# Retention, routed experts and a dense block on one core: where the query decay is multiplied in, which banks the transposes own, when the embedding is normalised, and how tiles are grouped

## The chip, the core and the metric

The kernel runs on one core of a Trainium2 chip. The core's engines run their own instruction queues in order: TensorE (PE, with its weight loads PEld), VectorE (DVE), ScalarE (ACT), GpSimd (POOL) and SyncE (SP, which here only issues transfers). An instruction starts when those ahead of it on its engine are done and the semaphores that it waits on have been raised. The metric is the time of one execution on the device in microseconds (us), as a median of several runs.

## The reference

Three stages follow each other. Stage one is a retention layer without softmax, for 4 batches, 8 heads, 576 positions and a head size of 64. The score of query position i and key position j is multiplied by a decay, gamma of the head to the power i - j:

```
scores = scale * np.matmul(q, k.transpose(0, 1, 3, 2))
gamma = 1.0 - 2.0 ** (-5.0 - np.arange(H, dtype=np.float32))
Dmat = np.where(rel >= 0, gamma[:, None, None] ** rel[None, :, :], 0.0)
ret = scores * Dmat[None, :, :, :]
return np.matmul(ret, v).astype(np.float32)
```

Its output, 2304 rows of 512, goes to stage two, which sends each row to one of 8 experts: the row and the 8 expert embeddings are normalised, the logits are their products divided by tau, the largest picks the expert, and its softmax weight scales the row's result `relu(x @ w1[e]) @ w2[e]`. Stage three is a dense block over all rows, `elu(x @ w_in) @ w_out`, whose weights come as float64.

## The kernel before, in words

**Decay as two factors.** gamma ** (i - j) is split into gamma ** i on the query and gamma ** -j on the key. Two constant tables of 5 position groups by 8 heads, `gq` and `gk`, hold them.

**Units and tiles.** The first stage runs over ten units (`UNITS`), each a pair of rows of work: per pair of batches four units of 256 positions (two tiles of 128 rows of output, two "slots") and one remnant unit (positions 512 to 575 of both batches, one tile, one slot). In units 0 to 9 the remnants are 4 and 9. There are 18 tiles.

**What a unit does.** The loop over `u` near line 684 issues, in this order: POOL scales q and k of unit u+2 (`scale`, L276); SP loads q, k of unit u+4 and v of u+3 (`load`, L257, L261); PE multiplies the carried state (`carried`, L340) and the scores of the second slot (`scores`, L315), DVE masks them (L320); PE transposes slot 0 of q and k of the next unit (`transposes`, L290), ACT copies each out of PSUM (L298); PE projects the previous unit's second tile (`xrows`, L404, "xa") with an identity matrix that also carries the expert embeddings, so that 128 columns are the row itself and 8 are logits; a pump of small DVE steps for the routing; transposes of slot 1; the product with v (`values`, L353), copied by ACT (L359, "xT"); the next unit's first scores; the state update (`summed`, L373, DVE L380 to L386); the projection of the unit's first tile; again a pump.

**PSUM.** Eight banks: `sc0`, `sc1` one each; `T`, `X`, `Y` two each. `T` holds a pair, q's transpose in its first bank and k's in its second, and also half of the projections; it has one buffer.

**Evicting a projection.** With tag `T` ACT copies the row (L416) and the logits (L418) and DVE sums the logits (L408); with tag `Y` DVE does both (L421, L408). SP stores the row in DRAM (L429) and ACT sums its squares for the norm (L441).

**Routing.** Tiles form four groups (`GROUPS`, 5 5 5 3). When a group's last tile is projected, two generators of small DVE steps (`expert_steps`, L473 to L534, and `gate_steps`, L445 to L562) are put into the pump, which stops at each `STEP`: a PE product "rp" (L490) in the one, an ACT exponential "ex" (L549) in the other. POOL then builds selection tables (L572 to L575) for each tile of a finished group. The last group is handled after the loop, in a serial tail up to the first product of the experts (L944).

**Start.** Before the loop, DVE scales unit 0, PE transposes it, ACT squares the embeddings (L625), DVE normalises them (L445 to L631), PE computes the first scores and state, and `emb_end` (L641) swaps halves of the embeddings (L645) and transposes them into the projection's matrix (L650).

**Rest.** From the first expert product to the end PE works through experts and the dense block with float32 operands split in two parts; the change does not touch that.

Of the kernel before, what the change touches and what calls it, by code (L numbers as in the profile page):

```python
# [17 lines left out]
P = 128  # L18
# [22 lines left out]
GROUPS = [(0, 5), (5, 5), (10, 5), (15, 3)]  # L41
# [4 lines left out]
for _n, _w in (("gq", 5 * H), ("gk", 5 * H), ("id", 2 * NT), ("w8", 8), ("base", 8), ("lim", NE * NK), ("i24", 24),  # L46
               ("i128", P), ("mask0", P), ("mask1", P), ("maskr", 64), ("lower", P)):
    COL[_n] = (_o, _o + _w)
    _o += _w
# [4 lines left out]
def constants():  # L54
# [10 lines left out]
    put("gq", (g[None, None, :] ** at[:, :, None] / 8.0).reshape(P, -1))  # L65
# [18 lines left out]
def tile_kernel(ctx: ExitStack, tc: tile.TileContext, q, k, v, emb, tau, w1, w2, w_in, w_out, const, out):  # L84
# [156 lines left out]
    rhsx = [st.tile([P, KD, P + NE], F32, name=f"rhsx{j}") for j in range(2)]  # L241
# [39 lines left out]
    def transposes(u, s_):  # L281
        if u >= NU or s_ not in slots_of(u):
            return
        if s_ == 0:
            tT[u] = (a2.tile([P, 4, 2, P], F32, tag="qTs", name=f"qT{u}"), a2.tile([P, 4, 2, 2, 64], F32, tag="kTs", name=f"kT{u}"))
        pair = ps.tile([P, 2, 512], F32, tag="T", name=f"qkT{u}_{s_}")
        for j, nm in enumerate("qk"):
            pt = pair[:, j].rearrange("p (r b i) -> p r b i", r=4, b=2)
# [3 lines left out]
            if j:  # L292
# [101 lines left out]
    def xrows(n, tag):  # L394
# [5 lines left out]
        xa = ps.tile([P, 2, 512], F32, tag=tag, name=f"xa{n}")  # L400
        W = P + NE
        for pr in range(4):
            for u, b, p0, w in where[n]:
                nc.tensor.matmul(xa[p0:p0 + w, pr // 2, (pr % 2) * W:(pr % 2 + 1) * W], xTs[u][b][:, pr, :w], rhsx[b][:, pr, :], start=True, stop=True)  # L404
        xav = xa[:, :, :2 * W].rearrange("p a (b w) -> p a b w", b=2)
        xs = xss[n] = a2.tile([P, 2, 2, P], F32, tag="xs", name=f"xs{n}", bufs=3)
        def logits(src):
            vec.tensor_reduce(out=gt[gi]["lg"][:, n - g0], in_=src, axis=AX.XY, op=ALU.add)  # L408

        le = xav[:, :, :, P:]  # L410
        if n == NT - 1:
            logits(le.rearrange("p a b e -> p e a b"))
            for a in range(2):
                nc.scalar.copy(out=xs[:, a], in_=xav[:, a, :, :P])
        elif tag == "T":
            nc.scalar.copy(out=xs, in_=xav[:, :, :, :P])  # L416
            lt = a2.tile([P, 2, 2, NE], F32, tag="lt", name=f"lt{n}")
            nc.scalar.copy(out=lt, in_=le)  # L418
            logits(lt.rearrange("p a b e -> p e a b"))
        else:  # L420
            vec.tensor_copy(out=xs, in_=xav[:, :, :, :P])  # L421
            logits(le.rearrange("p a b e -> p e a b"))
        b, c = TILES[n]
# [4 lines left out]
        for p0, p1, t0, eng in spans:  # L428
            eng.dma_start(out=xd[t0:t0 + p1 - p0, :], in_=xs[p0:p1].rearrange("p a b w -> p (a b w)"))  # L429

    xss = {}
# [5 lines left out]
    def squares(n):  # L437
        gi = grp_of[n]
        g0 = GROUPS[gi][0]
        sq = a2.tile([P, 2, 2, P], F32, tag="sq", name=f"sq{n}", bufs=1)  # L440
        nc.scalar.activation(out=sq, in_=xss[n], func=AF.Square, accum_out=gt[gi]["ss"][:, n - g0:n - g0 + 1])  # L441
# [148 lines left out]
    gcols = COL["gk"][1]  # L590
# [8 lines left out]
    for kk in range(KD):  # L599
        pool.tensor_copy(out=rhsx[0][:, kk, :P], in_=ident)  # L600
        for j in range(2):
            pool.tensor_copy(out=rhsx[1][:, kk, 64 * j:64 * j + 64], in_=ident[:, 64 - 64 * j:P - 64 * j])
# [3 lines left out]
    nc.scalar.dma_start(out=em, in_=emb)  # L606
    nc.scalar.dma_start(out=rtau, in_=tau.partition_broadcast(P))
    nc.sync.dma_start(out=ct[:, gcols:], in_=const[:, gcols:CSMALL])
    load(1, "v")
    load(2, "qk")  # L610
    scale(0)
    scale(1)
    for s_ in range(2):
# [7 lines left out]
    e1 = st.tile([NE, DM], F32, name="e1")  # L621
    es = st.tile([NE, 4], F32, name="es")

    def emb_steps():
        nc.scalar.activation(out=e1, in_=em, func=AF.Square, accum_out=es[:, 0:1])  # L625
        vec.reciprocal(out=rtau, in_=rtau)
        yield
        yield from norm_steps(es[:, 0:1], es[:, 1:2], es[:, 2:3])
        vec.reciprocal(out=es[:, 3:4], in_=es[:, 2:3])
        yield  # L630
        vec.tensor_scalar(out=e1, in0=em, scalar1=es[:, 3:4], scalar2=rtau[:NE, 0:1], op0=ALU.mult, op1=ALU.mult)  # L631
        yield

    for _ in emb_steps():
        pass
    scores(0, 0)
    summed(0)
    load(2, "v")
    load(3, "qk")

    def emb_end():  # L641
        pe = ps.tile([P, 2, KD, NE], F32, tag="Y", name="pemb")
        swap = st.tile([NE, KD, 2, 64], F32, name="swap")
        for j in range(2):
# [828 lines left out]
```

## Time and profile before

| what | us |
|---|---|
| median of 3 runs (786.06, 789.69, 790.55) | 789.69 |
| the profiled execution, whole | 785.31 |
| the profiled execution, span of the trace | 783.2 |
| PE busy in the span | 721.8 (92%) |
| DVE busy | 584.4 (75%) |
| ACT busy | 454.3 (58%) |
| POOL busy | 252.0 (32%) |

The profiled execution's time is 2.1 us longer than its span; what is before the first and after the last instruction stays. Busy shares are means over stages with different limits, so the first stage is read by itself: start of the span to about 167.6 us, where the first expert product begins. [...] In a row of the timeline, the bracket gives the time that the engine sat idle before the instruction, and what released it.

### The profile page before, as it was taken

What the parts mean: (1) busy time and instruction counts of PE and PEld (TensorE: products, weight loads), DVE (VectorE), ACT (ScalarE), POOL (GpSimd) and SP (SyncE); (2) the same over time, 40 slices, a digit from 0 to 9 for tenths busy, and PEclk for the clock granted to TensorE, in tenths of its full rate; (3) what the DMA queues carried; (4) which work ended last, traced back from release to release, by engine and by line L of the source; (5) the groups of instructions that cost most, each with busy time, mean ns of one, the idle gap of its engine ahead of it and who ended that gap; (6) DMA issues with size and microseconds to landing.
All of it is one profiled execution on the core that took longest, in us unless ns stands there. A gap on an engine that the chain in (4) does not pass through costs nothing.

```text
span 783.2 us, 15397 instructions
## 1 busy us (share of the span) xinstructions
PE 721.8 (92%) x5882; PEld 663.9 (85%) x5882; DVE 584.4 (75%) x917; ACT 454.3 (58%) x704; POOL 252.0 (32%) x370
## 2 busy tenths in 40 slices
PE   5687768589999999999899999999999999999996
PEld 5576667469999999998898899988999898989995
DVE  3335655577778879986888989998778998777773
ACT  2144434335565666565667766787665777676662
POOL 4314634341399124110052232227212324421103
PEclk8799889889999999999999999999999999999999
DMA  9575824157879999989733322114412123322102
GB/s 258 114 216 151 217 82 163 56 157 247 291 267 297 328 292 290 303 293 333 239 133 104 115 91 92 57 55 161 162 54 72 63 82 108 105 61 77 28 28 80
DMA packets 101794, 123.78 MB, mean 158 GB/s; under 512 B 12202, under 2 KB 71886, under 8 KB 101718
## 3 DMA queue, kind: packets, MB, share of 16 engines
q1 hardware_dynamic: 97430, 111.71, 45.6%
q0 software_dynamic: 3104, 9.83, 3.7%
q10 hardware_dynamic: 1184, 1.24, 0.6%
q8 instruction: 47, 0.77, 0.4%
q14 instruction: 29, 0.24, 0.1%
HBM read 99.91 MB, written 22.85 MB: 157 GB/s over the span
## 4 chain that ended last, share of the span: by engine, by line
issue 24%; PE 16%; POOL 9%; DVE 4%; DMA 1%; ACT 1%; POOLq 0%; ACTq 0%; DVEq 0%
PE o L229 6%; PE X L229 3%; PE Y L229 3%; PE h L229 2%; POOL out_dram L1385 2%; POOL qs L1187 2%; POOL qs L1186 2%; POOL qs L1184 2%; PE acc L961 2%; POOL qa L1185 1%; DMA ra<-in_moe_w_dram 1%; PE acc L963 1%; DVE hA L1350 0%; DVE glA L1358 0%; DVE xA L1347 0%
## 5 line engine op out<-in xcount | busy, mean ns | idle before, releaser
L1184 POOL TENSOR_TENSOR qs<-qa 128x256 f32<-128x256 f32 x24 | 22.4, 935 | 251.3 <-DMA qa<-wd 49.9
L229 PE MATMUL h<-xth,ha 128*128 128x332 f32 (+7 forms) x252 | 74.4, 311 | 1.0 <-DVEq L1094 1.0
L961 PE MATMUL acc<-hh,hb 128*128 128x342 f32 (+7 forms) x256 | 73.6, 304 | 1.7 <-ACT hh L947 1.7
L961 PE MATMUL acc<-hh,lb 128*128 128x342 f32 (+7 forms) x256 | 73.6, 303 | 0.3 <-DVE lb L203 0.3
L229 PE MATMUL h<-xtl,ha 128*128 128x332 f32 (+7 forms) x252 | 72.3, 303 | 0.0
L947 ACT ACTIVATE hh<-h 128x342 fp32r<-128x342 f32 (+7 forms) x64 | 27.1, 424 | 45.6 <-PE h L229 43.4
L320 DVE TENSOR_TENSOR A<-sc,ctbig 128x512 f32<-128x512 f32 (+1 forms) x36 | 22.1, 653 | 42.1 <-PE sc L315 42.1
L1337 ACT ACTIVATE rA<-hA 128x768 f32<-128x768 f32 x24 | 20.4, 848 | 55.3 <-DVE hA L1330 55.3
L203 DVE TENSOR_TENSOR la<-ra,ha 128x1024 fp32r<-128x1024 f32 x32 | 39.6, 1237 | 14.8 <-ACT ha L198 14.8
L1322 DVE TENSOR_TENSOR u<-Y,m 128x384 f32<-128x384 f32 x48 | 26.6, 553 | 31.9 <-PE Y L229 29.9
L961 PEld LDWEIGHTS acc<-hh,hb 128*128 128x128 f32 x256 | 48.3, 189 | 2.0 <-ACT hh L947 2.0
L963 PE MATMUL acc<-hl,hb 128*128 128x342 f32 (+7 forms) x256 | 46.8, 305 | 2.5 <-DVE hl L948 2.5
L229 PEld LDWEIGHTS h<-xth,ha 128*128 128x128 f32 x252 | 47.5, 189 | 1.6 <-DVEq L1094 1.3
L961 PEld LDWEIGHTS acc<-hh,lb 128*128 128x128 f32 x256 | 48.3, 189 | 0.6 <-DVE lb L203 0.6
L229 PEld LDWEIGHTS h<-xtl,ha 128*128 128x128 f32 x252 | 47.5, 189 | 0.0
L203 DVE TENSOR_TENSOR lb<-rb,hb 128x1024 fp32r<-128x1024 f32 x32 | 39.7, 1242 | 9.5 <-ACT hb L198 9.4
L229 PE MATMUL h<-xth,la 128*128 128x332 f32 (+7 forms) x252 | 45.6, 303 | 0.0
L888 POOL DMA_INDIRECT row<-xd,idsp x21 | 21.8, 1038 | 72.3 <-ACT xth L927 69.9
L1385 POOL DMA_INDIRECT out_dram<-ob,idc x18 | 20.3, 1126 | 68.4 <-ACT ob L1382 65.9
L963 PEld LDWEIGHTS acc<-hl,hb 128*128 128x128 f32 x256 | 38.9, 188 | 3.5 <-DVE hl L948 3.2
L229 PEld LDWEIGHTS h<-xth,la 128*128 128x128 f32 x252 | 38.5, 189 | 0.0
L198 ACT CAST hb<-rb 128x1024 fp32r<-128x1024 f32 x32 | 33.5, 1046 | 3.1 <-issue 2.2
(1689 smaller groups left out, 2346.5 us busy)
## 6 DMA issues: line engine op xcount, KB each, us to landing
ra<-in_moe_w_dram SPq DMA_DIRECT2D x31, 512.0 KB
rb<-in_moe_w_dram SPq DMA_DIRECT2D x31, 512.0 KB
qb<-wd SPq DMA_DIRECT2D x48, 256.0 KB
draw<-in_moe_w_in_dram SPq DMA_DIRECT2D x16, 512.0 KB
draw<-in_moe_w_out_dram SPq DMA_DIRECT2D x16, 512.0 KB
wd<-db SPq DMA_DIRECT2D x32, 256.0 KB
qa<-wd SPq DMA_DIRECT2D x24, 256.0 KB
qa<-wd SPq DMA_DIRECT2D x48, 128.0 KB
```

Source lines behind the costliest of these rows:

```text
L198: nc.scalar.copy(out=hi, in_=src)
L203: nc.vector.tensor_tensor(out=lo, in0=src, in1=hi.bitcast(F32), op=ALU.subtract)
L229: nc.tensor.matmul(o, l, r, start=first and n_ == 0, stop=last and n_ == len(seq) - 1, skip_group_check=True)
L320: vec.tensor_tensor(out=t[:, :, :w], in0=sc[j][:, :, :w], in1=m.unsqueeze(1).to_broadcast([P, 4, w]), op=ALU.mult)
L888: pool.indirect_dma_start(out=t[:m].rearrange("p k w -> p (k w)"), out_offset=None, in_=xd[:, :], in_offset=bass.IndirectOffsetOnAxis(ap=i ...
L947: nc.scalar.activation(out=hh, in_=hp[:, :c], func=AF.Relu)
L961: nc.tensor.matmul(acc[d][:, :c], w[d][w_], hh, start=f == 0 and w_ == 0, stop=False)
L963: nc.tensor.matmul(acc[d][:, :c], w[d][0], hl, start=False, stop=f == 7)
L1184: pool.tensor_tensor(out=S1, in0=A21, in1=A22, op=ALU.add)
L1322: vec.tensor_tensor(out=S_[nm], in0=S_["Y"], in1=S_["m1"], op=ALU.add)
L1337: nc.scalar.activation(out=Q[n]["r" + z], in_=Q[n]["h" + z], func=AF.Relu, scale=-1.0)
L1385: ins = pool.indirect_dma_start(out=out[:, :], out_offset=bass.IndirectOffsetOnAxis(ap=idc[:, col:col + 1], axis=0), in_=ob, in_offset=None)
```

## The change

q is no longer multiplied with its decay before the transpose, only copied in the layout that the transposes read (`scale`; one copy for both slots in place of two multiplications). The decay of the query position is multiplied into the projected rows instead, head by head. For that each head gets its own 8 logit columns, so a projection has 2 * (64 + 8) = 144 columns in place of 136; DVE multiplies the projection while it takes it out of PSUM, for both tags, and sums 8 by 8 logits out of SBUF. ACT's copies of rows and logits go. Rows lie in SBUF with a gap of 8 values behind each head, so a stored row is 8 pieces of 256 bytes in place of one of 2048.

The tag `T` becomes two tags, `qT` and `kT`, of one bank each. The embeddings' square is issued ahead of the first transposes on ACT, their normalisation and swap ahead of the first masks on DVE. More constant products (14 and 8 in place of 8) stand between the first transposes. Groups are 5 5 4 4. In the last tile, half of the rows is scaled by ACT, half by DVE after the last group's first steps. The core of the diff:

```diff
-GROUPS = [(0, 5), (5, 5), (10, 5), (15, 3)]
+GROUPS = [(0, 5), (5, 5), (10, 4), (14, 4)]
...
-        for nm, s_ in [(nm, s_) for nm in "qk" for s_ in slots_of(u)] if u == 0 else [(nm, s_) for s_ in slots_of(u) for nm in "qk"]:
+        eng = vec if u == 0 else pool
+        m = len(slots_of(u))
+        eng.tensor_copy(out=scaled[u]["q"][:, :m].rearrange("p s h d -> p h s d"), in_=loaded[u]["q"][:, :, :m, :])
+        for s_ in slots_of(u):
             g_ = 2 * c + s_ if c >= 0 else 4
-            eng = vec if u == 0 else pool
-            eng.tensor_tensor(out=scaled[u][nm][:, s_], in0=loaded[u][nm][:, :, s_, :],
-                              in1=C("g" + nm)[:, g_ * H:(g_ + 1) * H].unsqueeze(2).to_broadcast([P, H, D]), op=ALU.mult)
+            eng.tensor_tensor(out=scaled[u]["k"][:, s_], in0=loaded[u]["k"][:, :, s_, :],
+                              in1=C("gk")[:, g_ * H:(g_ + 1) * H].unsqueeze(2).to_broadcast([P, H, D]), op=ALU.mult)
...
-        pair = ps.tile([P, 2, 512], F32, tag="T", name=f"qkT{u}_{s_}")
-        for j, nm in enumerate("qk"):
-            pt = pair[:, j].rearrange("p (r b i) -> p r b i", r=4, b=2)
+        for nm in which:
+            pt = ps.tile([P, 4, 2, 64], F32, tag=nm + "T", name=f"{nm}Tp{u}_{s_}")
...
+        if tag == "T":
+            xa = [ps.tile([P, 512], F32, tag=nm + "T", name=f"xa{nm}{n}") for nm in "qk"]
...
+        def times(eng, h, a, d):
+            eng.tensor_tensor(out=xs[:, h * a:h * (a + 1), d], in0=xa[a][:, :2 * W].rearrange("p (h w) -> p h w", h=h)[:, :, d],
+                              in1=gq[:, h * a:h * (a + 1)].unsqueeze(2).to_broadcast([P, h, len(range(D + NE)[d])]), op=ALU.mult)
...
         elif tag == "T":
-            nc.scalar.copy(out=xs, in_=xav[:, :, :, :P])
-            lt = a2.tile([P, 2, 2, NE], F32, tag="lt", name=f"lt{n}")
-            nc.scalar.copy(out=lt, in_=le)
-            logits(lt.rearrange("p a b e -> p e a b"))
+            for a in range(2):
+                times(vec, 4, a, slice(0, D + NE))
+            logits()
         else:
-            vec.tensor_copy(out=xs, in_=xav[:, :, :, :P])
-            logits(le.rearrange("p a b e -> p e a b"))
+            vec.tensor_tensor(out=xs.rearrange("p (a h) w -> p a h w", a=2), in0=pair[:, :, :2 * W].rearrange("p a (h w) -> p a h w", h=4),
+                              in1=gq.rearrange("p (a h) -> p a h", a=2).unsqueeze(3).to_broadcast([P, 2, 4, D + NE]), op=ALU.mult)
+            logits()
...
+                eng.dma_start(out=xd[t0:t0 + p1 - p0, :].rearrange("t (h d) -> t h d", h=H), in_=xs[p0:p1, :, :D])
...
+        if n == NT - 1:
+            late.append(lambda: (times(vec, 4, 0, slice(0, D)), store(), squares(n)))
...
     for s_ in range(2):
-        transposes(0, s_)
-    t = ps.tile([P, 512], F32, tag="sc1", name="warm1")
-    for _ in range(8):
-        nc.tensor.matmul(t[:, :P], oneb, oneb, start=True, stop=True)
+        transposes(0, s_, "q")
+    constant(14, "sc1")
+    for s_ in range(2):
+        transposes(0, s_, "k")
...
     steps(ge, 99)
+    late.pop()()
     steps(ge, 1)
```

PE's queue around the transposes of one unit before, with the semaphores that each instruction waits on (engine names; `qkT` is the pair of banks, `qs` and `ks` the scaled inputs, `xa` a projection, `A` a masked score):

```order
L290 MATMUL qkT_0_598<-ident,qs_348 128x128 [waits PE_49,Activation_49,Pool_49]
L290 MATMUL qkT_0_598<-ident,ks_349 128x128 [waits Activation_49,Pool_49]
L404 MATMUL xa_609<-rhsx_134,xT_0_451 128x136 [waits DVE_49]
L290 MATMUL qkT_1_618<-ident,qs_348 128x128 [waits Activation_49,Pool_49]
L290 MATMUL qkT_1_618<-ident,ks_349 128x128 [waits Activation_49,Pool_49]
L353 MATMUL xTp_557<-A_1_592,v_214 64x128 [waits DVE_49]
```

The same place in the changed kernel (`qTp` and `kTp` are the two single banks):

```order
L292 MATMUL qTp_0_609<-ident,qs_360 128x128 [waits DVE_49,Pool_49]
L292 MATMUL kTp_0_615<-ident,ks_361 128x128 [waits DVE_49,Pool_49]
L410 MATMUL xa_621<-rhsx_134,xT_0_464 128x144 x4
L292 MATMUL qTp_1_630<-ident,qs_360 128x128 [waits Activation_49]
L292 MATMUL kTp_1_636<-ident,ks_361 128x128 [waits Activation_49,Pool_49]
L355 MATMUL xTp_568<-A_1_603,v_208 64x128 [waits DVE_49]
```

The order is the same. The k transposes of slot 0 wait for DVE (which empties the bank of the projection before) and no longer for ACT; those of slot 1 wait for ACT's copy of slot 0 of their own input, one bank each.

DVE's queue in the last units before, from the masks of unit 8's second slot (`A_8`) to the first instruction of the last group's steps (`mx` of `lg_2103`); rows of the two generators that lie between are left out:

```order
L320 TENSOR_TENSOR A_8_2040<-sc_8_1_2021,ctbig 128x512
L421 COPY xs_2060<-xa_2055 128x512
L473 TENSOR_REDUCE mx_2117<-lg_1588 128x5
L320 TENSOR_TENSOR A_9_2174<-sc_9_0_2156,ctbig 128x4x64
L203 TENSOR_TENSOR la_2210<-ra_1797,ha_2209 128x1024
L408 TENSOR_REDUCE lg_2103<-xa_2213 128x8
L510 TENSOR_TENSOR pr_2238<-rp_2231,oh 128x40
L547 TENSOR_TENSOR ex_2123<-lg_1588,r_2122 128x40
L555 RECIPROCAL gate_2124<-gate_2124 128x5
L473 TENSOR_REDUCE mx_2286<-lg_2103 128x3
```

The same in the changed kernel (the third group's logits are `lg_1605`, the last group's `lg_2098`):

```order
L494 TENSOR_REDUCE mx_2014<-lg_1605 128x4
L322 TENSOR_TENSOR A_8_2081<-sc_8_1_2062,ctbig 128x512
L434 TENSOR_TENSOR xs_2104<-xa_2099,ct 128x576
L531 TENSOR_TENSOR pr_2115<-rp_2109,oh 128x32
L568 TENSOR_TENSOR ex_2020<-lg_1605,r_2019 128x32
L576 RECIPROCAL gate_2021<-gate_2021 128x4
L322 TENSOR_TENSOR A_9_2241<-sc_9_0_2223,ctbig 128x4x64
L204 TENSOR_TENSOR la_2277<-ra_1815,ha_2276 128x1024
L417 TENSOR_TENSOR xs_2290<-xaq_2280,ct 128x4x8
L494 TENSOR_REDUCE mx_2301<-lg_2098 128x4
L417 TENSOR_TENSOR xs_2290<-xaq_2280,ct 128x4x64
```

The third group's steps have moved from behind the last mask to ahead of unit 8's and unit 9's masks, and nothing of them is left between `la` and the last group's first step; one multiplication of the last tile has come in behind that group's first steps.

## Rows read from the trace of the kernel before

**Rows 1.** Busy time by stretch: PE, PEld, DVE, ACT, POOL, clock, DMA share.

```profile
20.90:39.30 18.40, 13.55 (x240) 11.40 (x240) 5.28 (x11) 3.47 (x6) 6.08 (x6) 0.72 0.45 100
39.30:147.70 108.40, 84.22 (x1895) 74.63 (x1895) 54.41 (x153) 45.06 (x104) 39.38 (x75) 0.92 0.55 157
167.60:783.20 615.60, 602.86 (x3512) 562.34 (x3512) 501.66 (x658) 397.72 (x578) 182.89 (x227) 1.00 0.49 160
```

**Rows 2.** Waits of PE up to 167.6 us: total us, times, longest.

```profile
PE qkT L290 <- ACT qT L298: 16.6, 15, 5.6
PE qkT L290 <- ACT kT L298: 2.2, 3, 0.8
```

**Rows 3.** Timeline of PE, unit 2: start, duration, instruction, idle before it.

```profile
54.42 0.66 PE L290 MATMUL qkT<-ident,qs 128*128 128x128 f32 x4
55.87 0.63 PE L290 MATMUL qkT<-ident,ks 128*128 128x128 f32 x4 [0.80 <-ACT qT L298]
...
58.70 0.63 PE L290 MATMUL qkT<-ident,ks 128*128 128x128 f32 x4 [0.80 <-ACT qT L298]
59.25 1.98 PE L353 MATMUL xTp<-A,v 64*64 64x128 f32 x64
```

**Rows 4.** Timeline of DVE and PE in the start.

```profile
7.88 1.29 DVE L276 TENSOR_TENSOR ks<-k,ct 128x512 f32<-128x512 f32 x2 [1.12 <-DMA k<-in_k_dram]
14.68 0.14 DVE L445 TENSOR_SCALAR es<-es 8x1 int32<-8x1 int32 x1 [5.43 <-ACT e L625]
15.69 1.16 PE L373 MATMUL kv<-v,ks 64*64 64x64 f32 x64
19.26 1.27 DVE L320 TENSOR_TENSOR A<-sc,ctbig 128x512 f32<-128x512 f32 x2
20.92 0.76 PE L340 MATMUL xTp<-qT,S 64*64 64x128 f32 x10 [4.06 <-DVE S L380]
36.06 1.32 DVE L645 COPY swap<-e 8x256 f32<-8x256 f32 x2
```

**Rows 5.** Timeline of units 3, 4 and 6: PE and the DVE steps ahead of it.

```profile
75.69 1.19 PE L404 MATMUL xa<-rhsx,xT 128*128 128x136 f32 x8 [3.45 <-ACT xT L359]
79.54 4.20 DVE L562 TENSOR_TENSOR gate<-gate,parts 128x5 f32<-128x5 f32 x1
107.36 1.00 DVE L453 SCALAR_TENSOR_TENSOR r<-r,ss 128x5 f32<-128x5 f32 x1
109.81 1.00 DVE L455 SCALAR_TENSOR_TENSOR y<-y,r 128x5 f32<-128x5 f32 x1
112.30 1.11 PE L290 MATMUL qkT<-ident,ks 128*128 128x128 f32 x4 [5.61 <-ACT qT L298]
113.34 3.69 PE L353 MATMUL xTp<-A,v 64*64 64x128 f32 x64
```

**Rows 6.** Groups of instructions up to 168 us: busy us, mean ns.

```profile
L276 POOL TENSOR_TENSOR qs<-q,ct 128x512 f32<-128x512 f32 x16 | 17.2, 1073 | 22.3 <-DMA q<-in_q_dram 8.2 <-issue 8.2 <-PE qkT L290 5.5
L600 POOL COPY rhsx<-ident 128x128 f32<-128x128 f32 x4 | 1.1, 284 | 0.1
L320 DVE TENSOR_TENSOR A<-sc,ctbig 128x512 f32<-128x512 f32 x32 | 20.6, 683 | 42.1 <-PE sc L315 42.1
```

**Rows 7.** Timeline of the tail: DVE and PE.

```profile
148.14 1.22 DVE L203 TENSOR_TENSOR la<-ra,ha 128x1024 fp32r<-128x1024 f32 x1 [2.34 <-ACT ha L198]
153.42 0.16 DVE L473 TENSOR_REDUCE mx<-lg 128x3 f32<-128x24 f32 x1
154.51 0.20 PE L490 MATMUL rp<-oh,lowb 128*128 128x24 bf16 x1 [6.51 <-DVE oh L483]
```

**Rows 8.** DMA queue of SP in 0:167.6, 103.5:107.5, 134:138: packets, MB, share.

```profile
q1 hardware_dynamic: 37760, 24.09, 52.5%
...
q1 hardware_dynamic: 1336, 1.02, 88.4%
...
q1 hardware_dynamic: 144, 0.26, 17.4%
```

More of the change, by code (lines that the diff above doesn't have):

```diff
@@ L399, in xrows @@
             small(gi, "lg", NE)
-        xa = ps.tile([P, 2, 512], F32, tag=tag, name=f"xa{n}")
-        W = P + NE
+        W = 2 * (D + NE)
+        if tag == "T":
+            xa = [ps.tile([P, 512], F32, tag=nm + "T", name=f"xa{nm}{n}") for nm in "qk"]
+        else:
+            pair = ps.tile([P, 2, 512], F32, tag=tag, name=f"xa{n}")
+            xa = [pair[:, a] for a in range(2)]
         for pr in range(4):
             for u, b, p0, w in where[n]:
-                nc.tensor.matmul(xa[p0:p0 + w, pr // 2, (pr % 2) * W:(pr % 2 + 1) * W], xTs[u][b][:, pr, :w], rhsx[b][:, pr, :], start=True, stop=True)
@@ L405, in xrows @@
[L405 to L410, printed above, removed]
+                nc.tensor.matmul(xa[pr // 2][p0:p0 + w, (pr % 2) * W:(pr % 2 + 1) * W], xTs[u][b][:, pr, :w],
+                                 rhsx[b][:, pr].rearrange("p j w -> p (j w)"), start=True, stop=True)
@@ L411, in xrows @@
         if n == NT - 1:
-            logits(le.rearrange("p a b e -> p e a b"))
             for a in range(2):
-                nc.scalar.copy(out=xs[:, a], in_=xav[:, a, :, :P])
+                times(vec, 4, a, slice(D, D + NE))
+            logits()
+            for h in range(4):
+                nc.scalar.activation(out=xs[:, 4 + h, :D], in_=xa[1][:, (D + NE) * h:(D + NE) * h + D], func=AF.Copy, scale=gq[:, 4 + h:5 + h])
         elif tag == "T":
-            nc.scalar.copy(out=xs, in_=xav[:, :, :, :P])
@@ L427, in xrows @@
             spans = [(0, 64, b * S + 512, nc.sync), (64, P, (b + 1) * S + 512, nc.scalar if n == NT - 1 else nc.sync)]
-        for p0, p1, t0, eng in spans:
-            eng.dma_start(out=xd[t0:t0 + p1 - p0, :], in_=xs[p0:p1].rearrange("p a b w -> p (a b w)"))
+        if n == NT - 1:
+            late.append(lambda: (times(vec, 4, 0, slice(0, D)), store(), squares(n)))
+        else:
+            store()
+    late = []
     xss = {}
@@ L620, in tile_kernel @@
     pool.tensor_copy(out=parts[:, :, :2], in_=C("id").rearrange("p (n two) -> p n two", two=2))
[L621 to L634, printed above, removed]
-        pass
+    vec.reciprocal(out=rtau, in_=rtau)
+    for _ in norm_steps(es[:, 0:1], es[:, 1:2], es[:, 2:3]):
+        pass
+    vec.reciprocal(out=es[:, 3:4], in_=es[:, 2:3])
+    vec.tensor_scalar(out=e1, in0=em, scalar1=es[:, 3:4], scalar2=rtau[:NE, 0:1], op0=ALU.mult, op1=ALU.mult)
+    swap = st.tile([NE, KD, 2, 64], F32, name="swap")
+    for j in range(2):
+        vec.tensor_copy(out=swap[:, :, j, :], in_=e1.rearrange("e (k j d) -> e k j d", k=KD, j=2)[:, :, 1 - j, :])
+    constant(8, "sc0")
     scores(0, 0)
     summed(0)
-    load(2, "v")
     load(3, "qk")
@@ L642, in emb_end @@
         pe = ps.tile([P, 2, KD, NE], F32, tag="Y", name="pemb")
-        swap = st.tile([NE, KD, 2, 64], F32, name="swap")
-        for j in range(2):
-            vec.tensor_copy(out=swap[:, :, j, :], in_=e1.rearrange("e (k j d) -> e k j d", k=KD, j=2)[:, :, 1 - j, :])
         for b, src in enumerate((e1, swap.rearrange("e k j d -> e (k j d)"))):
@@ L649, in emb_end @@
         for b in range(2):
-            vec.tensor_copy(out=rhsx[b][:, :, P:], in_=pe[:, b])
+            for j in range(2):
+                o = 64 * (j ^ b)
+                vec.tensor_copy(out=rhsx[b][o:o + 64, :, j, D:], in_=pe[o:o + 64, b])
     NG = len(GROUPS)
```

51 lines of the change are left out of this document (34 added, 17 removed).

## The prediction

> **What bounds the kernel now.** I read the page's slices first, then busy time by stretch [rows 1]. From 167.6 us to the end PE is busy 602.86 of 615.60 us at a granted clock of 1.00, and the change leaves that part as it is: it can only move as a block. So the time is decided before 167.6 us. There PE is busy 13.55 of 18.40 us in unit 0 (clock 0.72) and 84.22 of 108.40 us in units 1 to 9 (clock 0.92); no other engine is busier than half of it. The bound is PE's in-order queue with the waits in it, and the next view is the list of PE's waits [rows 2]: the longest sum is transposes waiting for ACT's copy of q's transpose, 16.6 us in 15 waits, and 2.2 us more for the copy of k's. The timeline of one unit [rows 3] shows what they are: after q's four transposes (54.42 + 0.66) PE stands 0.80 us until ACT has emptied the first bank of the pair, though k goes to the second, and again at 58.70. Last I read the three places with a long single wait: the start [rows 4], unit 6 [rows 5] and the tail [rows 7].
>
> **The change part by part.** The sum is against the profiled execution, 785.31 us, 4.4 us below the median of the runs shown (789.69); I add that difference at the end.
>
> *Start.* PE stands 4.06 us before its first carried product at 20.92, behind DVE [rows 4]. DVE does the embedding steps from 14.68 to the masks at 19.26, 4.58 us, because ACT squares the embeddings only after four transpose copies. In the changed kernel the square is first on ACT, so these steps follow DVE's scaling of k, which ends at 7.88 + 1.29 = 9.17. Taking their 4.58 us again and adding the swap, which moves ahead (1.32), they end at 15.1. The first scores on PE should come about 1.5 us earlier than before (transposes of one input follow each other while the other loads, but 14 more constant products stand there); the state product at 15.69 + 1.16 = 16.85 would end near 15.4. Masks (two of 683 ns) [rows 6] and the state copy then end near 16.7, and PE goes on at 16.7 in place of 20.9: 4.2 us. Bounds: nothing, if ACT's square waits long for its input; 6 us, if the steps run without the company of POOL's multiplications. The swap then no longer stands in front of the first projection; I count 0.4 us for that, against two more small copies.
>
> *Waits of the transposes.* With single banks k's transposes do not wait for ACT's copy of q's, and the second slot's wait for a copy that began one transpose and (mostly) one projection earlier. Rows 2 hold 18.8 us in 18 waits; 5.6 us of it is unit 6's special case, two in the start lie on loads that are hidden otherwise, three in unit 0 are worth 2.4 us. For the units that leaves 2 waits of 0.8 us in a unit of two slots, three in unit 5, which has no projection between. I count 1.6 us each in units 1, 2 and 7, 2.4 in unit 5, 0.8 in unit 6: 8.0 us. In units 3, 4 and 8 something else ends later, so the gain there is not counted by waits (next two parts).
>
> *POOL's shorter scaling.* POOL's two multiplications of q (1073 ns each) [rows 6] become one copy of 1024 values. The nearest copy, 128 values in 284 ns, gives at most 8 * 284 = 2.3 us and, if most of it is a fixed part, about 1.2; I take 1.2, since the multiplications of 512 values take four times that of 128 copied. DVE steps with two inputs in SBUF stretch while POOL runs: L562 takes 4.20 us in unit 4, L453 and L455 1.00 us each in unit 6 [rows 5], on five values. One POOL instruction less of four shortens that by about 0.8 us. In unit 3 PE's 3.45 us wait, and in unit 4 the masks behind L562, end 0.8 us earlier: 1.6 us in all. Bound: nothing, if the copy costs as much as what it replaces.
>
> *Unit 6.* PE stands 5.61 us in front of k's transposes, because the copy it waits for is queued on ACT behind an exponential that waits for the stretched DVE steps; then it runs at half clock (3.69 us for a product that takes 1.98 in unit 2) [rows 3, 5]. After the change k's transposes and the product with v go first; the next that needs ACT's copies are unit 7's first scores. The DVE steps end about 1.3 us earlier, so the copies are there at about 111.4 and these scores start then, in place of the end of the product at 113.34 + 3.69 = 117.0. Of 5.3 us net, 0.8 is counted above: 4.5 us. Bounds: 2 us (the stretch is as before and PE falls to half clock again) to 6.
>
> *Tail.* Before, the third group's steps fill DVE between `la` (ends 148.14 + 1.22 = 149.36) and the last group's first step at 153.42: 4.06 us, on which PE waits 6.51 us [rows 7]. With groups of 5 5 4 4 they lie in units 7 to 9. They are not free there: in unit 8 the exponential now stands on ACT ahead of the copies of the product with v, which eats unit 8's 0.8 us and 0.3 more; in unit 9 eight gate steps stand ahead of the masks, 1.0 us. In the tail come the late multiplication (between the half and the whole of a mask's 683 ns; 0.4), two multiplications of logits (0.3) and a wait for the squares behind the late half (0.3). 4.06 - 1.3 - 1.0 leaves 1.8; I take 1.7 us, bounds -1 to 4.
>
> *What it adds.* Each projection has 144 in place of 136 columns: 8 matmuls of 286 ns or so, 0.064 us a tile, 18 tiles, 1.2 us, all on PE. DVE takes over ACT's nine evictions: two multiplications of 288 values out of PSUM, by the masks' row 683 * 288 / 512 = 0.38 to 0.68 us each, I take 0.45, so 0.9 us in nine units. It hides behind PE's next carried product and scores (about 1.9 us before the bank is wanted again), since DVE is idle there; if DVE comes late, the waits of rows 2 come back in part. For the other nine tiles a copy of 512 becomes a multiplication of 576, under 0.1 us. ACT loses its copies and sits on no path for it.
>
> *Stores.* A row of 2 KB becomes 8 pieces of 256 bytes. In 134:138 [rows 8] 144 packets, nearly all of 2 KB, took 17.4% of 16 engines' 4 us, 11.1 us, 77 ns each. In 103.5:107.5 1336 packets took 56.6 us; about 248 are of 2 KB, which leaves 34 ns for a piece of 256 bytes (loads of v's remnant mostly). A tile's store then takes 1024 * 34 / 16 = 2.2 us of the DMA engines in place of 0.6; 18 tiles add 28 us to 52.5% of 167.6 = 88 us. The stage has room, loads run two units ahead, and only the last store has a reader close by, some 7 us later: I count nothing. [...]
>
> Sum: start 4.2 + 0.4, unit 0 2.4, units 8.0, POOL 1.6, unit 6 4.5, tail 1.7, less 1.2: 21.6 us. 785.31 - 21.6 = 763.7; plus 4.4 for the median: **768 us**.
>
> **The rivals.**
>
> *Half of it.* The waits removed are replaced by others: DVE, which gets 0.9 us more in a unit and all masks, becomes late for the transposes' bank or for the masks, ACT's copies stand behind squares that wait for DVE, and the early start is held by POOL. For it: units 3, 4 and 6 are already held by DVE [rows 5]. Against it: in units 1, 2, 5 and 7 DVE is about half busy. Half of units and of unit 6, 3 us at the start, none in the tail: 3 + 1.6 + 4 + 2.3 - 1.2 = about 10 us, 779 us.
>
> *The clock stays up.* The clock was 0.72 in 20.90:39.30 [rows 1], after PE had stood. If the denser start holds the upper level, 13.55 us busy at 0.72 become 9.8, 3.8 us less; units 1 to 9 at 0.92 hold another 6.7, of which 1.7 are in unit 6's sum; perhaps half of the rest. Together about 6 us more: 762 us.
>
> *Stores bind, slower.* If a 256-byte write costs twice the 34 ns, a store takes 4.35 us, 3.7 more than before, 67 us over 18 tiles. 88 + 67 = 155 us of queue time, plus about 10 in which nothing may be issued, puts the last store at 165 in place of 152 us; the gather of the experts' first rows waits for all of them, so the stage ends 13 us later: 803 us. It decides from 88 + 18 x = 128 (the shortened stage without its tail), x = 2.2 us a store or 46 ns a packet. For it: one unit's loads and stores already come near the unit's length. Against it: loads of that size at 34 ns.
>
> *The change does not do what it says.* PE's waits for ACT could stay through another shared bank. The order of its queue speaks against it: k's first transposes wait for DVE and POOL only. About 786 us.
>
> **How the numbers follow.** The forecast 0.55 (own range 763 to 774), half 0.22, clock 0.15, stores 0.06, no effect 0.02. What a measurement of this kernel can tell from no change is about 0.5%, 4 us. Of the half case 0.18 is faster by more, 0.03 is within: faster 0.55 + 0.18 + 0.15 = 0.88, same 0.05 with most of the case without effect, slower 0.07. The range takes in the clock case with some room and the half case with some: 757 to 784.
>
> **What would show it.** Right: no wait of PE's transposes for ACT near 0.8 us and a sum under 4 us in place of 18.8; the first carried product before 18 us; no 5.6 us wait in unit 6; the first expert product between 141 and 152 us and the rest unchanged at 615.6. Wrong: PE waiting for DVE in front of transposes or masks with as much in sum (half case); a busy share of the queue near 1 up to the tail and gathers that wait for the last store (stores); the stretch after the first expert product longer than before.

## The result, and the profile after

The changed kernel took 760.42 us (median of 4 runs, 754.80 to 762.59); the kernel before, run beside it, 789.06. The ratio of their times is 0.963, 95% interval 0.957 to 0.969. Run a second time, in a comparison of its own, it took 759.75 us (6 runs), 0.963 (0.960 to 0.966). The forecast was 768 us in a range of 757 to 784: the direction and the range held, the gain of 28.6 us is 7.0 more than the 21.6 of the sum.

Two executions were profiled, of 754.8 and of 760.5 us. What follows calls them the first and the second profile. The first product of the experts, at 167.57 us before, comes at 140.63 in the first and at 145.79 in the second: the same program differs by 5 us in the first stage alone. A difference of 1 to 3 us in one place of one trace is therefore no finding by itself.

Busy time by stretch in the first profile (columns as in [rows 1]: length, busy PE, PEld, DVE, ACT, POOL, granted clock as a share of full speed, DMA share); the stretches are unit 0, units 1 to 9, and from the first expert product to the end:

```profile
18.30:32.86 14.56, 11.10 (x241) 9.55 (x241) 5.06 (x12) 3.29 (x6) 5.63 (x6) 0.94 0.75 180
32.86:122.50 89.64, 78.04 (x1891) 71.48 (x1892) 64.34 (x189) 37.60 (x86) 38.93 (x86) 0.97 0.74 188
140.63:753.00 612.37, 602.87 (x3512) 562.36 (x3512) 501.81 (x658) 397.86 (x578) 184.37 (x227) 1.00 0.49 161
```

Against [rows 1], unit 0 is 3.8 us shorter, units 1 to 9 are 18.8 us shorter, and the rest is 3.2 us shorter with the same PE busy time. PE's waits in the first stage (total us, times, longest; `xaq` and `xak` are the two halves of a projection, `pids` the tail's products with the selection tables):

```profile
PE xaq L410 <- ACT xT L361: 5.0, 3, 3.1
PE pids L848 <- DVE At L845: 3.9, 2, 2.5
PE rp L511 <- DVE oh L504: 3.2, 1, 3.2
PE sc L317 <- ACT qT L300: 2.8, 1, 2.8
...
PE qTp L292 <- ACT qT L300: 1.2, 3, 0.7
...
PE kTp L292 <- ACT kT L300: 0.7, 1, 0.7
```

The 18.8 us of [rows 2] are 1.9 us now. In the timeline of unit 1 (PE: start, duration, instruction) the transposes of q and k follow each other without a bracket; those of unit 2, where [rows 3] had 0.80 us twice, do so too (45.15 to 47.50):

```profile
35.49 0.66 PE L292 MATMUL qTp<-ident,qs 128*128 128x128 f32 x4
35.98 0.60 PE L292 MATMUL kTp<-ident,ks 128*128 128x128 f32 x4
36.42 1.15 PE L410 MATMUL xa<-rhsx,xT 128*128 128x144 f32 x8
37.40 0.60 PE L292 MATMUL qTp<-ident,qs 128*128 128x128 f32 x4
37.84 0.60 PE L292 MATMUL kTp<-ident,ks 128*128 128x128 f32 x4
38.37 1.98 PE L355 MATMUL xTp<-A,v 64*64 64x128 f32 x64
```

What stands in place of the 5.61 us wait of [rows 5] is a shorter wait, in unit 6 (second line), and its like in unit 3 (first line), which was 3.45 us before [rows 5] (PE, then unit 3's ACT):

```profile
63.59 0.76 PE L410 MATMUL xaq<-rhsx,xT 128*128 128x144 f32 x4 [3.12 <-ACT xT L361]
93.96 1.10 PE L317 MATMUL sc<-qT,kT 64*64 64x128 f32 x32 [2.76 <-ACT qT L300]
```

```profile
62.83 0.24 ACT L570 ACTIVATE ex<-ex 128x40 f32<-128x40 f32 x1 [4.97 <-DVE ex L568]
62.97 1.05 ACT L361 COPY xT<-xTp 128x512 f32<-128x512 f32 x2
```

In unit 3 PE waits for a copy that ACT could have made some 2.5 us earlier, when the product with v had ended (60.47): ahead of it in the queue stands the gate's exponential, idle until DVE has its input. The new or changed operations (busy us, mean ns), answering [rows 6]:

```profile
L276 POOL COPY qs<-q 128x1024 f32<-128x1024 f32 x7 | 7.3, 1037 | 11.9 <-DMA q<-in_q_dram 10.5 <-DVE A L322 1.4
...
L417 DVE TENSOR_TENSOR xs<-xak,ct 128x288 f32<-128x288 f32 x9 | 4.1, 453 | 0.6 <-PE xak L410 0.5
...
L434 DVE TENSOR_TENSOR xs<-xa,ct 128x576 f32<-128x576 f32 x8 | 6.0, 750 | 1.9 <-PE xa L410 1.1 <-ACT kT L300 0.8
```

The tail (DVE and PE), answering [rows 7]: from the end of `la` to the last group's first step there are now 0.5 us (before, 4.06), and PE waits 3.24 us in place of 6.51.

```profile
123.62 1.22 DVE L204 TENSOR_TENSOR la<-ra,ha 128x1024 fp32r<-128x1024 f32 x1 [2.07 <-ACT ha L199]
125.38 0.19 DVE L494 TENSOR_REDUCE mx<-lg 128x4 f32<-128x32 f32 x1
126.53 0.21 PE L511 MATMUL rp<-oh,lowb 128*128 128x32 bf16 x1 [3.24 <-DVE oh L504]
```

SP's DMA queue in the stage up to 140.6 us, answering [rows 8]:

```profile
q1 hardware_dynamic: 53440, 24.09, 68.0%
```

That is 95.6 us of the 16 engines' time, 8 more than before, where I had expected 28 more.

### The profile page after: what moved, and what is told of

Read it like the earlier page. It is cut to its first block, busy times and chain, and to the rows that moved or that the text cites. A ratio compares the mean times of both kernels' runs of the same rounds, so it can differ in the third digit from the quotient of the medians.

```text
span 753.0 us, 15419 instructions
## 1 busy us (share of the span) xinstructions
PE 715.6 (95%) x5897; PEld 661.8 (88%) x5897; DVE 589.7 (78%) x939; ACT 447.8 (59%) x688; POOL 242.7 (32%) x352
## 4 chain that ended last, share of the span: by engine, by line
PE 27%; issue 14%; DVE 8%; POOL 4%; ACT 2%; DMA 1%; SPq 0%; POOLq 0%; ACTq 0%; DVEq 0%
PE o L230 12%; PE X L230 7%; PE Y L230 5%; PE h L230 2%; PE acc L987 1%; DMA draw<-in_moe_w_in_dram 1%; POOL out_dram L1411 1%; POOL qs L1212 1%; PE acc L989 1%; POOL qa L1211 1%; DVE hA L1376 1%; POOL qs L1213 1%; POOL qs L1210 1%; DVE glA L1384 1%; DVE xA L1373 1%
## 5 line engine op out<-in xcount | busy, mean ns | idle before, releaser
L204 DVE TENSOR_TENSOR la<-ra,ha 128x1024 fp32r<-128x1024 f32 x32 | 39.1, 1223 | 14.9 <-ACT ha L199 14.9
```

Source lines behind the costliest of these rows:

```text
L204: nc.vector.tensor_tensor(out=lo, in0=src, in1=hi.bitcast(F32), op=ALU.subtract)
```

## The experiments

Besides the kernel before, eleven kernels ran, the changed one twice. All ratios are to the kernel before on the same chip, with 95% intervals; "first expert product" is from the one profiled execution.

| kernel | median us | ratio | first expert product |
|---|---|---|---|
| before (787.8 to 790.2 beside the others) | 789.06 | 1 | 167.57 |
| changed, first / second profile | 760.42 / 759.75 | 0.963 / 0.963 (0.960 to 0.966) | 140.63 / 145.79 |
| single banks alone | 767.56 | 0.973 (0.967 to 0.978) | 147.99 |
| changed, with the pair of banks | 782.48 | 0.989 (0.986 to 0.993) | 165.63 |
| early embedding alone | 786.16 | 0.997 (0.994 to 1.001) | 167.78 |
| changed, without constant products | 764.59 | 0.968 (0.962 to 0.974) | 150.36 |
| changed, two multiplications on POOL | 761.37 | 0.967 (0.963 to 0.971) | 139.85 |
| changed, groups 5 5 5 3 | 760.37 | 0.967 (0.962 to 0.971) | 143.44 |
| before, waits filled | 786.71 | 0.998 (0.995 to 1.001) | 164.20 |
| changed, later exponential | 753.89 | 0.957 (0.954 to 0.960) | 132.56 |
| changed, stores twice, same place | 789.76 | 1.002 (0.999 to 1.005) | 171.78 |
| changed, stores twice, other place | 759.72 | 0.961 (0.956 to 0.966) | 143.21 |

**Single banks alone, and the change without them.**

```diff
-        pair = ps.tile([P, 2, 512], F32, tag="T", name=f"qkT{u}_{s_}")
         for j, nm in enumerate("qk"):
-            pt = pair[:, j].rearrange("p (r b i) -> p r b i", r=4, b=2)
+            pt = ps.tile([P, 4, 2, 64], F32, tag=nm + "T", name=f"{nm}Tp{u}_{s_}")
...
```

> The kernel before with one part of the change: every group of four transposes, and each half of a projection that went into the transposes' pair, has a single bank (the copies on ScalarE are made bank by bank, two small ones more a projection). Theory (the prediction's steps): the 18.8 us of waits for ScalarE's copies fall under 4 us; unit 0 gains 2.4, the units 8.0, unit 6 some 2 to 4.5 of its 5.6 us wait; the first expert product comes near 155 in place of 167.6 us, the run 12 to 15 us faster. Rival (the waits are replaced by others, behind VectorE and the slower scaling on GpSimd): half of that, 6 us, first expert product near 161.5.

> The changed kernel with the pair of banks back, everything else of the change kept (in the start q's and k's transposes stand by input again, with the 14 constant products behind them). Theory: the waits for ScalarE's copies are back at 16 to 19 us in sum, the first expert product comes 11 to 14 us later than the 140.6 us of the changed kernel, near 153, the run near 773 us. Rival (copying q and the other parts carry the gain): 5 us or less, first expert product near 145.

Measured: the banks alone take 2.7% (21 us) off, the rest of the change alone 1.1% (8 us). Busy time of the stretch from the first carried product of unit 0 to that of unit 9, before, banks alone, pair, and changed (one line each, in this order):

```profile
20.92:142.31 121.39, 93.10 (x2013) 82.17 (x2013) 56.99 (x149) 45.39 (x101) 44.45 (x76) 0.89 0.54 151
```

```profile
16.82:122.93 106.11, 90.29 (x2014) 82.51 (x2014) 57.04 (x149) 45.99 (x118) 47.57 (x82) 0.90 0.68 184
```

```profile
18.79:141.94 123.15, 92.49 (x2018) 81.93 (x2018) 64.90 (x186) 40.66 (x86) 40.72 (x82) 0.90 0.62 155
```

```profile
18.30:116.96 98.66, 85.11 (x2018) 77.64 (x2018) 65.14 (x187) 39.06 (x86) 41.12 (x82) 0.97 0.77 194
```

Length less PE busy is PE's idle time: 28.3, 15.8, 30.7 and 13.6 us. With the pair it is all back, with the banks alone 12.5 of the 14.7 us that the change takes off are gone. PE's waits for the copies of the transposes say the same; up to the first expert product they are, with the pair:

```profile
PE qkT L293 <- ACT qT L301: 16.8, 16, 5.0
...
PE qkT L293 <- ACT kT L301: 2.0, 3, 0.7
```

and with the banks alone, the first of them in front of unit 7's scores:

```profile
PE sc L314 <- ACT qT L297: 3.6, 1, 3.6
...
PE qTp L289 <- ACT qT L297: 0.4, 1, 0.4
```

The theory held, and its rivals (half, or little) fell. Both runs moved by more than it had put, 21 us for 12 to 15 and 22 for 11 to 14. Part of this is in the start, on which it had put nothing: with the banks alone the first carried product comes at 16.82 in place of 20.92 us. ACT's square of the embeddings stands behind the four transpose copies, these end earlier, and the embedding steps and masks of [rows 4] follow (before, then banks alone):

```profile
13.94 0.62 ACT L625 ACTIVATE e<-em 8x512 f32<-8x512 f32 x1
```

```profile
11.21 0.62 ACT L625 ACTIVATE e<-em 8x512 f32<-8x512 f32 x1
```

Of the 4.1 us 0.9 are an earlier load of k, 1.8 the transposes without their waits, and 1.4 embedding steps that take less, in one trace each. The banks carry the change.

**Early embedding alone.**

```diff
...
+    nc.scalar.activation(out=e1, in_=em, func=AF.Square, accum_out=es[:, 0:1])
     scale(0)
...
```

> The kernel before with the embedding's square, norm and swap ahead of the scores, and nothing else. Theory (the prediction's step): the first carried product comes 4.2 us before its 20.92 us, and 0.4 us are gained behind it; run 4 to 5 us faster. Rival (what the changed kernel's trace suggests: TensorE's own chain at half clock, transposes, scores, state product, sets the start): 2 to 2.6 us, first carried product near 18.3 to 19.

Measured: the first carried product came at 16.99 in place of 20.92 us, 3.9 earlier, near the theory; unit 1 began 7.3 us earlier (32.00 for 39.31). None of it reached the first expert product in that execution: unit 1 took 17.77 us for 13.21, with a stall of 2.78 us and products at half clock behind it (granted clock 0.50 in 48:52). In the runs it is worth 2.1 us, in an interval that includes nothing.

**No constant products in the start.**

```diff
-    constant(14, "sc1")
...
-    constant(8, "sc0")
```

> The changed kernel without the 14 and the 8 constant products in the start. Theory (the constant products hold the clock until unit 0): the granted clock of unit 0 falls from 0.93 to near the 0.72 of the kernel before, unit 0 takes 2 to 3 us longer, the run 2 to 4 us slower than the changed kernel. Rival (the clock of unit 0 comes from its own products following each other without waits): clock of unit 0 at 0.9 or more, the start about 1 to 2 us earlier by the products left out, the run the same or 1 us faster.

Measured: neither theory as put. The first carried product came at 15.40 us, 2.9 before the first profile's, unit 0 had a clock of 0.94 and took 14.54 us as in the first profile, so the products do not hold unit 0's clock. But the transposes ran at half clock from 7.71 us on (1.11 us for 0.63, granted clock 0.50 in 8:12), and units 1 to 6 took 76.6 us against 64.2 and 69.2 in the two profiles of the changed kernel. Of the 12.4 us to the first, 6.0 are stalls of the kind that the last section shows. The run, 764.6 us, can't be told from the changed kernel's.

**Two multiplications on POOL; groups.**

```diff
...
+                eng.tensor_tensor(out=scaled[u]["q"][:, s_], in0=loaded[u]["q"][:, :, s_, :],
+                                  in1=oneh.unsqueeze(2).to_broadcast([P, H, D]), op=ALU.mult)
...
```

> The changed kernel with two multiplications of q by ones on GpSimd in each unit but the first, in place of the copy. Theory (the prediction's step): GpSimd's longer work stretches VectorE's steps again, unit 3 and unit 4 are 0.8 us longer each, 1.6 us in all, and little elsewhere. Rival: with single banks GpSimd's end is also what the next transposes wait for, so more units lose, 4 us or more. Second rival: the two multiplications end as late as the copy does, nothing.

```diff
-GROUPS = [(0, 5), (5, 5), (10, 4), (14, 4)]
+GROUPS = [(0, 5), (5, 5), (10, 5), (15, 3)]
```

> The changed kernel with tile groups of 5 5 5 3 in place of 5 5 4 4. Theory (the prediction's step): the tail has the third group's steps again, 4.06 us of VectorE less what the tail and units 8 and 9 gain back (1.3 + 1.0): first expert product 1.7 us later, the run 1 to 3 us slower. Rival: the steps hide in the tail behind what else stands there; same time.

Measured: neither run can be told from the changed kernel's. The medians are within 2 us of its two, the ratios 0.4 points above them, with intervals of 0.3 to 0.6 points to each side, so a cost of some 3 us, or none, fits both. In the traces the waits say what was expected: with the multiplications unit 3's wait is 3.8 us (2.8 to 3.1 in five other traces of the change whose loads are not held up), unit 6's 3.6 (2.7 to 2.8), unit 6 is 2.4 us longer in all than in the first profile, unit 4 is not longer; with the old groups unit 9 and the tail take 26.8 us for 23.7 and unit 8, without the exponential, 7.8 for 8.6: 2.3 net for the 1.7 expected.

**Waits filled.**

```diff
+            if not j and not s_ and u:
+                f = ps.tile([P, 2, 512], F32, tag="Y", name=f"fill{u}")
+                for _ in range(12):
+                    nc.tensor.matmul(f[:, 0, :P], oneb, oneb, start=True, stop=True)
```

> The kernel before with 12 small constant products on TensorE between q's and k's transposes of the first slot of each unit but the first, where TensorE stood 0.8 us in each unit; the copy is waited for as before. Theory (besides their own length the waits cost clock: the granted clock of units 1, 2, 5, 6 and 7 was 0.82 to 0.87 where the changed kernel has 0.93 to 1.00): filled waits raise the clock of these units and the stage gets 2 to 5 us shorter although no wait is removed. Rival (the waits cost their length alone): the same time, or 1 to 2 us longer by products that outlast the waits.

Measured: idle time in the stretch fell from 28.3 to 22.6 us and busy time rose from 93.1 to 97.0; the granted clock was 0.92 for 0.89. The run is the same (0.995 to 1.001). Filling a third of the waits gave nothing that can be measured. The theory's premise was also misread: before, units 1, 4, 5 and 6 had a clock of 0.82 to 0.87, but units 2 and 7 had 1.00. With the fill, of these four only unit 5 rose (0.87 to 1.00), and units 1 to 8 together have 0.92 as before. That the waits also cost clock is not borne out, though not excluded for those that were not filled.

**A later exponential.** In the loop, behind `values(u)`:

```diff
-        nc.scalar.activation(out=ex, in_=ex, func=AF.Exp)
+            later.append(lambda: nc.scalar.activation(out=ex, in_=ex, func=AF.Exp))
...
         values(u)
+        flush()
```

> The changed kernel with one more edit: the exponential of the first three groups stands on ScalarE's queue behind the two copies of the unit's product with v (and so behind the copies of the next unit's transposes), in place of ahead of them. Theory (TensorE's waits of 3.1 us in unit 3, 2.8 in unit 6 and 1.4 in unit 8 are ScalarE's queue standing behind an exponential that waits for VectorE): the three waits go, the first expert product comes 5 to 7 us before the 140.6 us of the changed kernel, the run 5 us faster (ratio to the kernel before near 0.957). Rival (VectorE's own chain, which the exponential waits for, also holds the masks and evictions of these units): 1 to 2 us, with new waits for VectorE in units 3, 6 and 8.

Measured: 753.89 us, 6 us below the changed kernel and the fastest here. Unit 3 takes 8.16 us for 10.59, unit 6 11.12 for 13.33, unit 8 7.89 for 8.57: 5.3 us, as the theory had it. ACT and PE of unit 3 in its trace: the copy goes first, the exponential's wait for DVE holds up no copy, and 0.69 us are left of PE's wait.

```profile
59.19 1.07 ACT L361 COPY xT<-xTp 128x512 f32<-128x512 f32 x2 [2.67 <-PE xTp L355]
61.49 0.24 ACT L577 ACTIVATE ex<-ex 128x40 f32<-128x40 f32 x1 [1.23 <-DVE ex L574]
```

```profile
59.82 0.76 PE L410 MATMUL xaq<-rhsx,xT 128*128 128x144 f32 x4 [0.69 <-ACT xT L361]
```

**The changed kernel again.**

> The changed kernel as it is, once more. Theory (the clock of the start differs from run to run: in its first profile the first carried product came at 18.3 us with transposes at 1.1 us, in three kernels with the same start at 14.0 us with transposes at 0.63 to 0.66): first carried product at 14 us and the first expert product near 138 us, with a stage behind it of 612 to 619 us; run 760 us. Rival (the start at half clock belongs to the changed kernel): 18.3 and 140.6 us again.

Measured: the rival's start, with the first carried product at 18.02, and the first expert product of neither, at 145.79. The start at half clock, read from the length of its transposes (1.09 us for 0.63), is not the program's alone, though: the five kernels with the same start in other runs (POOL, groups, exponential, both stores) had it at 13.98 to 14.17. The first transposes in the first profile, and in the kernel with the old groups:

```profile
6.33 1.09 PE L292 MATMUL qTp<-ident,qs 128*128 128x128 f32 x4 [0.81 <-DVE qs L276]
```

```profile
6.22 0.63 PE L292 MATMUL qTp<-ident,qs 128*128 128x128 f32 x4 [0.71 <-DVE qs L276]
```

**Stores twice.** First to the same place, then to one of their own (the edit of the second, its long line shortened):

```diff
-                eng.dma_start(out=xd[t0:t0 + p1 - p0, :]...
+                for x in (xd, xd2):
+                    eng.dma_start(out=x[t0:t0 + p1 - p0, :]...
```

> The changed kernel with each tile's store issued twice (the same bytes to the same place). Theory (the prediction's step: the stores in pieces of 256 bytes are hidden; the trace has some 19 ns for such a packet, 1.2 us of the 16 engines for a store): the queue is busy 22 us more of 141, nothing waits for it, the first expert product moves by under 1 us, the run is the same. Rival (the stores share the queue with loads that units wait for): some units 1 us longer, first expert product 4 us later or more, the run 4 us slower.

> The changed kernel with each tile's store issued twice, the second time to a place of its own, so that no store waits for another's landing as in the run before. Theory (stores in pieces of 256 bytes are hidden; the run before lost 31 us in the stage because each second store held SyncE's queue until the first had landed): the queue is busy some 10 to 22 us more, the first expert product comes within 1 to 2 us of the 140.6 and 145.8 us of the changed kernel, the run at 760 us. Rival (the pieces themselves take the room that loads and buffers need): first expert product 5 us later or more, waits for VectorE behind a tile buffer, the run 765 us or more.

Measured: the first of the two asked the wrong question. A second store of the same bytes waits on SP until the first has landed (six issues held the queue for 15.5 us from 88.42 on). SP's waits of this kind up to the first expert product (total us, times, longest):

```profile
SPq L441 <- DMA xd<-xs: 67.4, 19, 6.3
```

So loads and later stores came late, and the stage was 31 us longer than in the first profile. With a place of its own the doubled store costs nothing that can be measured: 759.72 us, with this row for 0:140:

```profile
q1 hardware_dynamic: 71664, 28.68, 82.7%
```

The second profile of the changed kernel has 53440 packets and 68.7% there. 18224 packets more took 14.0% of 16 * 140 us, 17 ns each.

## Why the prediction was right, and where it was short

*Single banks (unit 0 2.4, units 8.0, unit 6 4.5).* Right in mechanism: the waits went, the kernel with the pair has them back. The size was near: banks alone took 15.3 us off units 0 to 8, for 14.9. Of unit 6's wait 2.8 us are left, in front of unit 7's scores, as the sum had it. What it put at nothing, as lying on loads, are the two waits in the start: with the banks alone, the transposes without them were worth 1.8 of the 4.1 us there.

*The units together.* The gains of the start, of units 0 to 8 and of unit 9 with the tail, in us (the 1.2 us for wider columns are taken off in the sum alone):

| | start | 0 | 1 | 2 | 3 | 4 | 5 | 6 | 7 | 8 | 9, tail | sum |
|---|---|---|---|---|---|---|---|---|---|---|---|---|
| forecast | 4.2 | 2.8 | 1.6 | 1.6 | 0.8 | 0.8 | 2.4 | 5.3 | 1.6 | 0 | 1.7 | 21.6 |
| first profile | 2.6 | 3.8 | 2.8 | 1.9 | 0.9 | 2.2 | 3.1 | 5.9 | 2.1 | 0.1 | 1.6 | 26.9 |
| second profile | 2.9 | 2.7 | 1.8 | 1.0 | 0.9 | -0.6 | 2.8 | 5.9 | 2.7 | 0.0 | 1.7 | 21.8 |

How close the sum of the second comes is luck in part. In units 0 to 8 my terms had 15.2 us of idle time and 1.7 of clock; PE's idle time fell by 14.7 us in the first profile and 11.0 in the second, its busy time by 8.0 and 6.3.

*Start (4.2).* The step failed in its reason. I let DVE's embedding steps take their 4.58 us again; without POOL beside them the steps on `es` took 0.12 to 0.15 us each (before, beside POOL's multiplications, two of them 0.73 and 0.97) and the swap ended at 11.3, but PE was no earlier for it: its own chain (transposes, scores, state product) ends last, at 18.0 to 18.3 us with half-clock transposes (1.06 to 1.12 us in the first profile), just past the 18 that I had named as a sign, and at 14.0 otherwise. My 16.7 lies between the two, neither of which I foresaw. Early embedding and single banks also do not add up here: each alone brings the first carried product to 16.99 and 16.82 us. And the constant products, which I had set against the order of the transposes, are in this chain: without them it ends at 15.40, at half clock too.

*POOL (1.6).* The copy of 1024 values took 1.04 us, near the 1.2 taken. Against the kernel with the multiplications, unit 3 shows its 0.8 (wait 0.7, length 0.9), though its wait is only 0.3 us shorter than before; unit 4 shows nothing; unit 6, where I had not put it, shows 0.8 in the wait. In the run it can't be told from nothing.

*Tail (1.7).* 1.6 and 1.7 us with unit 9; 2.3, unit 8 included, by the kernel with the old groups.

*Evictions and stores.* 450 ns for 288 values and 750 for 576 as taken; the stores were over-sized by two (17 ns a packet, not 34) and are hidden, so the stores rival (803 us) is far from deciding: even the doubled queue is 82.7% busy. (Its limit of 46 ns a packet comes to 44 from its own figures.) No run shows a 256-byte write at twice 34 ns, on which that rival's sum rests; the stores to their own place showed 17 ns. Against 77 ns for 2 KB [rows 8] that is 1.8 times the time per byte, too little to matter here.

*What was short.* Two places. I left the time from the first expert product on as it was, 615.6 us; it took 612.4 and 612.9. PE's busy time there is the same, but two waits behind the hidden layer of an early expert, 1.73 and 2.52 us before, are one of 0.71 (1.22 in the second). Over the runs of all kernels this part took 612.4 to 618.9 us and its waits of this kind 0.6 to 4.8; the longer ones are mostly in kernels with the pair or without the full change. Why is open. The other is in the stage: its 26.9 us in the first profile are 5.3 more than the sum, its 21.8 in the second 0.2. The traces gain 30.2 and 24.5 us in all, the medians 28.6. Whether the 4.4 us that I added, by which the one profiled execution of before lay below its median, are a fault of the sum can't be said: the first profile lies 5.6 us below its own median, the second 0.8 above.

*The clock rival (762).* Its time is nearer to the result than the forecast's, and its sign is there: the clock of units 0 to 8 is 0.97 (second profile 0.95) for 0.89, and PE's busy time 8.0 (6.3) us less, of which I had counted 1.7. But the banks alone left it at 0.90 and filled waits at 0.92. The rest with the pair has 0.90 too. With the whole change it is 0.93 to 0.97 in six traces (both profiles, the multiplications, the old groups, the later exponential, stores to their own place), 0.92 without the constant products, and 0.87 where the doubled stores held up the loads. So neither part raised it by itself, each in the one trace that there is; what the two do together is open, and that the removed waits did it is not shown. The half case fell with the banks alone; that PE's waits stay fell with the rows.

## What to carry to other kernels

Two buffers that are always written and read one after the other should not be one tile: what waited here was the tile, not the bank (0.80 us a time in [rows 3]), and that was three quarters of the gain. Sum such waits over the stage and expect about their length: 18.8 us of waits before, and 21 us in the run with the banks alone, of which some came by way of another engine's queue in the start. In an in-order queue, put an operation whose input comes late behind the copies that another engine needs; here, with the exponential, that took 5.3 us off three units.

## What the runs showed of the hardware

**A stall at a fixed place of PE's instruction stream.** "issue" waits, in which PE waits for nothing that the profile shows, sit mostly inside the state product, between two of its 64 matmuls (first profile up to 140.63 us: 2.7 us in 4 waits there, 0.9 in one in front of a score). In unit 0's of the changed kernel, first and second profile, and of the kernel without the 22 constant products:

```profile
26.50 0.41 PE L375 MATMUL kv<-v,ks 64*64 64x64 f32 x15
27.51 0.97 PE L375 MATMUL kv<-v,ks 64*64 64x64 f32 x49 [0.59 <-issue]
```

```profile
25.25 0.41 PE L375 MATMUL kv<-v,ks 64*64 64x64 f32 x15
28.17 0.97 PE L375 MATMUL kv<-v,ks 64*64 64x64 f32 x49 [2.51 <-issue]
```

```profile
22.46 0.75 PE L375 MATMUL kv<-v,ks 64*64 64x64 f32 x37
24.89 0.68 PE L375 MATMUL kv<-v,ks 64*64 64x64 f32 x27 [1.68 <-issue]
```

The stall comes after 15 matmuls in both executions, and after 37 where 22 matmuls less stand ahead, so that in all three traces 349 matmuls are before it: it belongs to a place in the stream of instructions, not to data. The distance from one such stall to the next shows a grid. Busy time from a stall to the next, two rows without the constant products and one of the first profile:

```profile
40.59:54.64 14.05, 11.73 (x253) 10.91 (x254) 5.97 (x12) 4.62 (x10) 1.04 (x1) 0.88 0.78 190
54.65:77.78 23.13, 17.01 (x380) 15.46 (x379) 17.36 (x51) 8.37 (x20) 15.54 (x30) 0.93 0.75 193
```

```profile
52.15:81.86 29.71, 26.05 (x634) 23.77 (x634) 23.05 (x63) 13.11 (x29) 17.64 (x32) 0.94 0.82 204
```

253, 380 and 634 matmuls, with as many weight loads, are 2, 3 and 5 times some 127 of each, that is, multiples of some 253 instructions. In the DMA list of the first profile up to 140.63 us a queue named "instruction" moves 16 KB a packet:

```profile
q8 instruction: 19, 0.31, 1.0%
```

The stall's length differs from run to run; those in state products sum to 2.7, 5.1 and 10.4 us in these three. DMA's share in 40:41 of the last, in which such a stall ends, is 109%; in 40:41 of the first profile it is 129%, without a stall. That instructions come late is my guess from the even distances; no run took the stalls away, and their cause is not shown. There are 4 stalls in state products in either profile and 6 without the constant products, beside 19 packets of the queue named "instruction" in the first profile; over the runs one stall took 0.2 to 2.8 us. Such stalls can take up what a start gains: they are 7.7 us longer without the constant products than in the first profile, and 4.4 us longer with the early embedding alone than before (6.8 for 2.4), where the starts came 2.9 and 3.9 us earlier. That they do so each time is not shown.

**The clock's column in the start.** For 4:16 of the first profile it says 1.00, where transposes take 1.06 to 1.12 us that take 0.60 to 0.66 elsewhere. A third of this stretch, and one of the transposes in it:

```profile
8.00:12.00 4.00, 3.46 (x22) 3.00 (x22) 2.92 (x15) 1.06 (x3) 0.14 (x1) 1.00 1.18 307
```

```profile
8.13 1.12 PE L292 MATMUL qTp<-ident,qs 128*128 128x128 f32 x4 [0.71 <-ACT qT L300]
```

In 8:12 of the kernel before, with transposes as long, it says 0.57, and in 8:12 of the kernel without constant products 0.50. So column and durations disagree in the first profile, and "half clock" is read from the durations there.
